# A one-core attention and two-layer FFN kernel: two transpose groups of each head pair moved to another place in TensorE's order

## The chip, the cores and the metric

The kernel runs on one core of a Trainium2 chip. The metric is the device time of one execution in microseconds; the time of a kernel is the median of its runs.

## The reference

The attention takes 4 batches of 8 heads, 576 positions and a head size of 64. Its scores carry a decay made of the running sum of log f, and its mask is causal. Two dense layers follow it, in fp32 throughout.

```python
scores = scale * np.matmul(q, k.transpose(0, 1, 3, 2))
cum = np.cumsum(np.log(np.clip(f, 0.0001, 1.0)), axis=-1)
scores = np.where(causal, -1e9, scores + cum[:, :, :, None] - cum[:, :, None, :])
attn = np.exp(scores - np.max(scores, axis=-1, keepdims=True))
attn = attn / (np.sum(attn, axis=-1, keepdims=True) + 1e-09)
x = np.matmul(attn, v)                  # then (tokens 2304, model 512)
h = x @ w_in;  x = (h - np.tanh(h)) @ w_out
h = x @ w_in2; out = (h * (1 / (1 + np.exp(-h)))) @ w_out2
```

## The kernel before

The attention takes two heads at a time, a **pair**; there are 16 pairs (`NP`). The 576 queries of a head are cut into blocks of 128 (the last of 64), which makes 9 score tiles for a pair (`NTILE`): blocks 0 to 3 of either head, and the last 64 queries of both heads in one tile. The tiles are made in four **units**: unit 0 is blocks 0 and 1 of both heads, units 1 and 2 are blocks 2 and 3, unit 3 is the last queries.

For each pair there are these pieces of work:

- `scores(p, u)` is TensorE's matmuls of a unit, K rows 0 to 63 for one head beside rows 64 to 127 for the other (unit 3 uses all 128 rows). The result tile `s` has two buffers in PSUM, so the scores of a unit need the buffer that the scores two units earlier filled.
- `least` is VectorE's reading of one score tile (L671): it adds the mask, finds the row's least value and writes the scores to SBUF. `expo` is the exponential on ScalarE (L679). `guard` and `normalise` (L686, L690 on VectorE, L693 on GpSimd) divide three tiles by their row sums.
- `transposes(p, u)` turns the finished tiles of a unit on TensorE (L705) into PSUM tiles `t`, of which there are three buffers (`ps_t`); `evac(p, u)` copies these to the SBUF tile `ptf`, some on ScalarE and some on VectorE (L750).
- `values(p)` multiplies the turned tiles with v (L761), and `collect` copies the result to `x`.

The order on every engine is written out by hand. The loop at L897 goes through steps n, nine for a pair; `later(n, fn, ...)` books a piece of work for a step, and `run(n, fn)` at the step writes it out. Scores of pair p+1 are written in the steps 8 (unit 0, the step before the pair's first), 0, 4 and 6 of the pair's nine; the transposes of pair p, which run while pair p+1's scores are made, in step 4 (unit 0, booked at `n0 + 13`), 6 (units 1 and 3's tile, `n0 + 15`) and 8 (unit 2, `n0 + 17`), each evacuated one step later; `values(p)` in step 4 of pair p+2. Within a step the order is transposes, values, scores, then evacuations, `expo`, `collect`, `least`, `normalise`, and last the jobs that prepare the first FFN weights (`wjob`, from pair 3 on one job each in the steps 1, 3, 5 and 7, most of them on VectorE). An engine takes its instructions in the order in which they are written, so the order of the steps is also the order on each engine.

The attention takes the first 170 us or so; the FFN's projections follow, in which TensorE works without a break.

Of the kernel before, what the change touches and what calls it, by code (L numbers as in the profile page):

```python
# [41 lines left out]
def forgetting_attention_two_ffn(  # L42
# [163 lines left out]
    for s in range(2 * NSET):  # L206
        e, o, k = 2 * s + 2, 2 * s + 3, 6 * s
# [104 lines left out]
    for u, (l, s, b) in enumerate(units):  # L312
# [14 lines left out]
        if l and s == 0:  # L327
            k = 5 if b == 0 else 11
# [208 lines left out]
    def attention(first):  # L537
        with ExitStack() as actx:
# [19 lines left out]
            NP = B * NPAIR  # L558
# [108 lines left out]
            def least(t):  # L667
                p, h, i = t
                src, m, pt = sps.pop(t)
                mn = small.tile([P, 1], F32, tag="mn", name=f"mn{p}_{h}_{i}")  # L670
                nc.vector.tensor_tensor_reduce(  # L671
                    out=pt.rearrange("p (g c) -> p g c", g=2) if i == 4 else pt, in0=src, in1=m,
                    op0=ALU.add, op1=ALU.min, scale=-SCALE, scalar=3.0e38, accum_out=mn,
                )
                ptile[t] = (pt, mn)

            def expo(n):
                pt, mn = ptile[tiles[n]]
                nc.scalar.activation(  # L679
                    pt, pt, AF.Exp, bias=mn, scale=-1.0,  # L680
                    accum_out=sums[:, n // 3 % 5, n % 3, 0:1],
                )

            def guard(n):
                sm = rowsum[n // 3] = small.tile([P, 3], F32, tag="sm", name=f"sm{n}")
                nc.vector.tensor_reduce(sm, sums[:, n // 3 % 5], axis=AX.X, op=ALU.add)  # L686

            def normalise(n):
                sm = rowsum.pop(n // 3)
                nc.vector.reciprocal(sm, sm)  # L690
                for j in range(3):
                    pt, _ = ptile[tiles[n + j]]
                    nc.gpsimd.tensor_scalar(pt, pt, sm[:, j:j + 1], 1.0, ALU.mult, ALU.mult)  # L693

            def transposes(p, u):

                ptf = ptfs[p % 2]
                tps[p, u] = moves = []
                both = u == 1 and p < NP - 1

                def tile(j):
                    return ps_t.tile([P, 4, P], F32, tag="t", name=f"t{p}_{u}_{j}")

                def turn(t, k, pt, c):
                    nc.tensor.transpose(t[:, k], pt[:, c * P:c * P + P], ident)  # L705

                def move(eng, src, dst):
                    moves.append((nc.scalar.copy if eng == "A" else nc.vector.tensor_copy, dst, src))

                def square(i, c, n, t, k, eng):  # L710
                    for h in range(2):
                        for j in range(n):
                            turn(t, k + n * h + j, pts[h, i], c + j)
                    src, q = t[:, k:k + 2 * n], P * i + 448 * c
                    if n == 1:
                        return move(eng, src, ptf[:, :, q:q + P])
                    dst = ptf[:, :, q:q + 448 * n].rearrange("p h (c w) -> p h c w", w=448)[:, :, :, 0:P]
                    move(eng, src.rearrange("p (h c) w -> p h c w", h=2), dst)

                def last_four(t, eng):  # L720
                    for c in range(4):
                        turn(t, c, pt4[p % 2], c)
                    dst = ptf[:, :, 512:512 + 4 * 448].rearrange("p h (c w) -> p c h w", w=448)[:, :, :, 0:64]
                    move(eng, t.rearrange("p c (h w) -> p c h w", h=2), dst)

                def last_fifth(t, k, eng):
                    turn(t, k, pt4[p % 2], 4)
                    o = 448 * 4 + 512
                    move(eng, t[:, k].rearrange("p (h w) -> p h w", h=2), ptf[:, :, o:o + 64])

                pts = {t: ptile.pop((p,) + t)[0] for t in units[u]}
                if both:
                    ptile.pop((p, 2, 4))
                if u == 0:
                    square(1, 0, 2, tile(0), 0, "V")
                    square(0, 0, 1, tile(1), 0, "A")
                elif u < 3:
                    square(u + 1, 0, 2, tile(0), 0, "A")
                    t = tile(1)
                    square(u + 1, 2, u, t, 0, "V")  # L740
                    if both:
                        last_fifth(t, 2, "V")
                        last_four(tile(2), "A")
                else:
                    last_four(tile(0), "A")
                    last_fifth(tile(1), 0, "V")

            def evac(p, u):
                for fn, dst, src in tps.pop((p, u)):
                    fn(dst, src)  # L750
# [35 lines left out]
            def busy(t, count):  # L786

                for _ in range(count):
                    nc.tensor.matmul(out_t, t[:, 0:P], t[:, 0:512], start=True, stop=True)  # L789
# [25 lines left out]
            def later(n, fn, *a):  # L815
                due.setdefault(max(n, 0), []).append((fn, a))

            def run(n, *fns):
                for fn, a in due.get(n, []):
                    if fn in fns:  # L820
                        fn(*a)

            for p in range(1, NP):
                n0 = NTILE * (p - 1)
# [12 lines left out]
            for p in range(NP):  # L837
                n0 = NTILE * p
                for u, k in enumerate((-1, 0, 4, 6)):
                    if p + u:  # L840
                        later(n0 + k, scores, p, u)
                k = ends_.get(p, steps_)
                for u in range(4 if k[3] else 3):
                    later(n0 + k[u], transposes, p, u)
                    later(n0 + k[u] + 1, evac, p, u)
                later(n0 + k[4], values, p, [(0, 0), (64, 0), (64, 1), (64, 2), (64, 3), (64, 4)])
                later(n0 + k[4] + 1, collect, p, 0, 64)
                later(n0 + k[4] + 1, collect, p, 64, S)

            def has(n):  # L850
                return 0 <= n < N
# [45 lines left out]
            for n in range(N + NTILE + 1):  # L897
                if n % NTILE == 0:
                    run(n, scores)
                    run(n, transposes)  # L900
                    run(n, values)
                else:
                    run(n, transposes)
                    run(n, values)
                    run(n, scores)
                if n < NTILE - 1:
                    busy(kqs[0][:, 0], 2)
                run(n, evac)
                if has(n - 1):
                    expo(n - 1)  # L910
                run(n, collect)
                if n % 3 == 2 and has(n - 5):
                    guard(n - 5)
                if has(n):
                    least(tiles[n])
                if n % 3 == 2 and has(n - 5):
                    normalise(n - 5)
                run(n, load_kq, load_v, split, place_last, place_dec, place_dec_last)
                for fn, *a in ahead.get(n - N, []):
                    fn(*a)  # L920
# [3 lines left out]
    with tc.manual_schedule():  # L924
        slots = [slot_steps(sl) for sl in range(NSL)]
        attention(slots[0])
        for job in jobs(1, 1, LAST):
            wjob(*job)
        for slot in slots:
            for _ in slot:  # L930
                pass
        rest()
        for n in range(8 * (NSL - 2) + 2, len(halves)):
            project(n)
# [39 lines left out]
```

## Time and profile before

| | before |
|---|---|
| median of 3 runs | 937.5 us (937.47 to 937.91) |
| profiled execution | 937.38 us |
| its span, first to last instruction | 935.6 us |
| TensorE busy | 927.4 us, 99% of the span |
| VectorE, ScalarE, GpSimd busy | 729.6, 439.0, 174.0 us |
| granted TensorE clock | 1.00 |
| period of a pair in the attention | 9.89 us |

Read the table from the stage: TensorE is busy nearly the whole span, and in the attention VectorE, ScalarE and GpSimd are nearly as full. A pair's period is the distance between the first matmul of unit 2 in one pair and that in the next.

### The profile page before, as it was taken

To read this page: it belongs to the slowest core of one execution; us is meant where nothing else is said; L and a number is where in the kernel's file an instruction comes from. 1 tells how busy PE (TensorE), PEld (TensorE's weight loads), DVE (VectorE), ACT (ScalarE), POOL (GpSimd) and SP (SyncE) were. 2 spreads that over 40 slices of the span, in tenths; PEclk is the share of its full clock that TensorE was granted. 3 is DMA by queue.
4 is the path that set the end of the run, shared out by engine and by line. 5 is a ranking of instruction groups with operands and counts; after the bars stand their busy time and mean duration, and the time that the engine had idled before them with its cause. 6 is when DMAs were issued, how large, how long until landed. Compare 5 with 4: busy or idle time off the path is not lost.

```text
span 935.6 us, 14919 instructions
## 1 busy us (share of the span) xinstructions
PE 927.4 (99%) x5532; PEld 846.0 (90%) x5532; DVE 729.6 (78%) x1320; ACT 439.0 (47%) x790; POOL 174.0 (19%) x248
## 2 busy tenths in 40 slices
PE   8999999999999999999999999999999999999998
PEld 6777777799999999999999999888888989888887
DVE  7798998898888887888788998877776677664444
ACT  6889888666453424242424354645342334232311
POOL 8999998200000000000000011010000000000000
PEclk9999999999999999999999999999999999999999
DMA  5435451668457753775477337464875477436722
GB/s 166 148 97 173 141 158 57 259 235 325 192 204 282 274 196 133 286 273 201 143 272 280 139 144 281 180 257 171 326 271 170 177 269 255 142 126 232 255 83 102
DMA packets 45946, 188.89 MB, mean 202 GB/s; under 512 B 9456, under 2 KB 9712, under 8 KB 45840
## 3 DMA queue, kind: packets, MB, share of 16 engines
q1 hardware_dynamic: 45720, 187.77, 55.0%
q8 instruction: 44, 0.72, 0.3%
q14 instruction: 30, 0.25, 0.1%
q10 hardware_dynamic: 152, 0.15, 0.1%
HBM read 148.44 MB, written 38.34 MB: 200 GB/s over the span
## 4 chain that ended last, share of the span: by engine, by line
PE 95%; DVE 3%; issue 1%; ACT 1%; POOL 0%; DMA 0%; POOLq 0%; ACTq 0%
PE a L385 42%; PE h L417 34%; PE t L705 5%; PE s L658 5%; PE out_t L761 4%; PE s L650 2%; PE h L431 2%; DVE xt L267 0%; PE out L761 0%; PE out_t L789 0%; DVE xo L281 0%; DVE wl L193 0%; DVE t L438 0%; PE a L367 0%; DVE gl L460 0%
## 5 line engine op out<-in xcount | busy, mean ns | idle before, releaser
L417 PE MATMUL h<-xo,wh 128*128 128x384 f32 x1232 | 314.0, 335 | 0.0
L470 DVE TENSOR_TENSOR hs<-h,hs 128x384 f32<-128x384 f32 x308 | 170.8, 555 | 90.3 <-PE h L417 86.6
L417 PEld LDWEIGHTS h<-xo,wh 128*128 128x128 f32 x1232 | 225.5, 188 | 14.1
L447 ACT ACTIVATE t<-hs 128x768 f32<-128x768 f32 x88 | 74.6, 847 | 309.2 <-DVE hs L470 309.2
L417 PE MATMUL h<-xo,wl 128*128 128x384 f32 x616 | 206.8, 336 | 0.0
L385 PE MATMUL a<-gh,wh 128*128 128x384 f32 x384 | 128.5, 335 | 0.5 <-ACT x L399 0.5
L385 PE MATMUL a<-gh,wl 128*128 128x384 f32 x384 | 128.3, 334 | 0.0
L385 PE MATMUL a<-gl,wh 128*128 128x384 f32 x384 | 128.3, 334 | 0.0
L460 DVE TENSOR_TENSOR gl<-t,gh 128x768 fp32r<-128x768 f32 x96 | 91.6, 954 | 34.0 <-ACT gh L456 33.6
L417 PEld LDWEIGHTS h<-xo,wl 128*128 128x128 f32 x616 | 115.6, 188 | 0.0
L385 PE MATMUL a<-wh,gl 128*128 128x512 f32 x284 | 112.6, 396 | 0.0
L385 PE MATMUL a<-wl,gh 128*128 128x512 f32 x284 | 112.2, 395 | 0.0
L385 PE MATMUL a<-wh,gh 128*128 128x512 f32 x284 | 110.5, 389 | 0.0
L456 ACT CAST gh<-t 128x768 fp32r<-128x768 f32 x96 | 80.4, 838 | 34.1 <-DVE t L449 27.9
L281 POOL TENSOR_TENSOR xo<-xt,xo 128x768 fp32r<-128x768 f32 x3 | 6.2, 2073 | 426.6 <-ACT xo L280 426.6
L679 ACT ACTIVATE p<-p,mn 128x128 f32<-128x128 f32 (+3 forms) x128 | 71.2, 558 | 16.9 <-DVE mn L671 14.2
L693 POOL TENSOR_SCALAR p<-p,sm 128x128 f32<-128x128 f32 (+3 forms) x128 | 72.7, 584 | 7.4 <-DVE sm L690 6.9
L385 PEld LDWEIGHTS a<-gh,wh 128*128 128x128 f32 x384 | 72.1, 188 | 1.1 <-ACT x L399 0.9
L385 PEld LDWEIGHTS a<-gl,wh 128*128 128x128 f32 x384 | 72.1, 188 | 0.0
L385 PEld LDWEIGHTS a<-gh,wl 128*128 128x128 f32 x384 | 72.1, 188 | 0.0
L671 DVE CUSTOM_DVE_ANT_0 p<-s,mask 128x128 f32<-128x128 f32 (+3 forms) x128 | 59.7, 480 | 14.3 <-PE s L658 14.2
L401 DVE TENSOR_TENSOR x<-a,x 128x768 f32<-128x768 f32 (+2 forms) x60 | 57.1, 951 | 9.2 <-PE a L385 9.1
(104 smaller groups left out, 1390.9 us busy)
## 6 DMA issues: line engine op xcount, KB each, us to landing
xo<-xd SPq DMA_DIRECT2D x126, 768.0 KB
xd<-xo SPq DMA_DIRECT2D x42, 768.0 KB
raw<-w_in SPq DMA_DIRECT2D x32, 512.0 KB
raw<-w_out SPq DMA_DIRECT2D x32, 512.0 KB
kqraw<-kq SPq DMA_DIRECT2D x16, 608.0 KB
vraw<-v SPq DMA_DIRECT2D x16, 320.0 KB
out<-ob SPq DMA_DIRECT2D x6, 512.0 KB
out<-ob SPq DMA_DIRECT2D x5, 256.0 KB
```

The source lines that it names most:

```text
L385: nc.tensor.matmul(dst, w, m, start=first and r == 0, stop=last and r == 2)
L401: nc.vector.tensor_tensor(total, acc, total, ALU.add)
L417: nc.tensor.matmul(dst, w[:, ks], m[:, k], start=k == 0 and r == 0, stop=k == 1 and r == 2)
L447: nc.scalar.activation(t, hs[h], AF.Silu if l else AF.Tanh)
L456: nc.scalar.copy(gh, hs[h])
L460: nc.vector.tensor_tensor(gl, hs[h], rd(gh), ALU.subtract)
L470: nc.vector.tensor_tensor(to, p, s, ALU.add)
L658: nc.tensor.matmul(s[:, h, c:c + n], a[half(h), q], b[half(h), 0:n], start=r == 0, stop=r == 3,)
L671: nc.vector.tensor_tensor_reduce(out=pt.rearrange("p (g c) -> p g c", g=2) if i == 4 else pt, in0=src, in1=m, op0=ALU.add, op1=ALU.min, sc ...
L679: nc.scalar.activation(pt, pt, AF.Exp, bias=mn, scale=-1.0, accum_out=sums[:, n // 3 % 5, n % 3, 0:1],)
L693: nc.gpsimd.tensor_scalar(pt, pt, sm[:, j:j + 1], 1.0, ALU.mult, ALU.mult)
L705: nc.tensor.transpose(t[:, k], pt[:, c * P:c * P + P], ident)
```

## The change

For every pair but the last two, the transposes of unit 0 are booked in the step of unit 1's (`k[1]`, step 6) under another name, `turn_first`, which `run` writes behind the evacuations of that step. For this the evacuation of unit 1 comes one step earlier, into the step of its own transposes, and the evacuation of unit 0 goes to the step after, two steps later than before.

```diff
+            def turn_first(p, u):
+                transposes(p, u)
+
@@
                 for u in range(4 if k[3] else 3):
+                    if p < NP - 2 and u < 2:
+                        later(n0 + k[1], (turn_first, transposes)[u], p, u)
+                        later(n0 + k[1] + 1 - u, evac, p, u)
+                        continue
                     later(n0 + k[u], transposes, p, u)
                     later(n0 + k[u] + 1, evac, p, u)
@@
                 run(n, evac)
+                run(n, turn_first)
                 if has(n - 1):
                     expo(n - 1)
```

Instructions are the same in number and kind; their order differs. In the rows below, `s5_2` is the scores of pair 5, unit 2, `t4_0_1` the second PSUM tile of pair 4's unit 0 transposes, `p5_2` and `pt4` the score tiles in SBUF, `mn` the row minima, `out_0` and `out_t` the results of the values.

TensorE, at the end of pair 5's unit 1 scores, before:

```order
L658 MATMUL s5_1_992<-de1_108 128x384 x2
L705 MATMUL t4_0_0_1033<-ident_203,p4_0_791 128x128 x4
L705 MATMUL t4_0_1_1038<-ident_203,p4_0_791 128x128 x2
L761 MATMUL out_0_3_1041<-ptf1_105,vraw3_669 64x64 x2
L761 MATMUL out_t_113<-ptf1_105,vraw3_669 64x512 x2
L761 MATMUL out_t_113<-ptf1_105,vraw3_669 64x448 x2
```

and with the change:

```order
L658 MATMUL s5_1_992<-de1_108 128x384 x2
L764 MATMUL out_0_3_1033<-ptf1_105,vraw3_669 64x64 x2
L764 MATMUL out_t_113<-ptf1_105,vraw3_669 64x512 x2
L764 MATMUL out_t_113<-ptf1_105,vraw3_669 64x448 x2
L764 MATMUL out_t_113<-ptf1_105,vraw3_669 64x320 x2
```

The values of pair 3 now stand directly behind the scores; the six transposes of pair 4's unit 0 are gone from between them.

TensorE, at the end of pair 5's unit 3 scores, before:

```order
L650 MATMUL s5_3_1098<-de1_108,lq1_110 128x288
L705 MATMUL t4_2_0_1118<-ident_203,p4_2_886 128x128 x4
L705 MATMUL t4_2_1_1123<-ident_203,p4_2_886 128x128 x4
L658 MATMUL s6_0_1128<-kqs6_990 128x128 x6
L658 MATMUL s6_0_1128<-de0_107 128x128 x2
```

and with the change:

```order
L650 MATMUL s5_3_1088<-de1_108,lq1_110 128x288
L705 MATMUL t4_0_0_1101<-ident_203,p4_0_791 128x128 x4
L705 MATMUL t4_0_1_1106<-ident_203,p4_0_791 128x128 x2
L705 MATMUL t4_2_0_1118<-ident_203,p4_2_878 128x128 x4
L705 MATMUL t4_2_1_1123<-ident_203,p4_2_878 128x128 x4
L658 MATMUL s6_0_1128<-kqs6_990 128x128 x6
L658 MATMUL s6_0_1128<-de0_107 128x128 x2
```

The six transposes now stand here, between the last queries' scores and the transposes of unit 2.

VectorE, from the reading of pair 5's unit 2 scores (`s5_2`) to that of its unit 3 (`s5_3`), before:

```order
L671 ISA p5_2_1055,mn5_0_3_1108<-s5_2_1054,mask_152 128x512
L671 ISA mn5_0_3_1108 128x1
L750 COPY ptf0_106<-t4_1_1_1089 128x2x128
L750 COPY ptf0_106<-t4_1_1_1089 128x2x64
L671 ISA p5_2_1055,mn5_1_3_1115<-s5_2_1054,mask_152 128x512
L671 ISA mn5_1_3_1115 128x1
L179 TENSOR_TENSOR ws0_0_1016<-ws0_0_1016 128x256
L686 TENSOR_REDUCE sm48_1147<-sums_157 128x3
L671 ISA pt4_1_112,mn5_2_4_1149<-s5_3_1098,mask4_159 128x576
L671 ISA mn5_2_4_1149 128x1
```

and with the change:

```order
L753 COPY ptf0_106<-t4_1_1_1079 128x2x128
L753 COPY ptf0_106<-t4_1_1_1079 128x2x64
L671 ISA p5_2_1047,mn5_0_3_1110<-s5_2_1046,mask_152 128x512
L671 ISA mn5_0_3_1110 128x1
L753 COPY ptf0_106<-t4_0_0_1101 128x2x2x128
L671 ISA p5_2_1047,mn5_1_3_1115<-s5_2_1046,mask_152 128x512
L671 ISA mn5_1_3_1115 128x1
L179 TENSOR_TENSOR ws0_0_1016<-ws0_0_1016 128x256
L686 TENSOR_REDUCE sm48_1147<-sums_157 128x3
L671 ISA pt4_1_112,mn5_2_4_1149<-s5_3_1088,mask4_159 128x576
L671 ISA mn5_2_4_1149 128x1
```

The copies of `t4_1_1` now stand ahead of both readings of `s5_2` rather than between them, and the copy of `t4_0_0` has come between the two (before it stood two tiles earlier, between the two readings of `s5_1`). On ScalarE the copies of `t4_1_0` and `t4_1_2` likewise stand one exponential earlier, and that of `t4_0_1` two later.

## Rows read from the trace of the kernel before

**Rows 1.** The page, part 1: engine, busy us, share of the span, instructions.

```profile
PE 927.4 (99%) x5532; PEld 846.0 (90%) x5532; DVE 729.6 (78%) x1320; ACT 439.0 (47%) x790; POOL 174.0 (19%) x248
```

**Rows 2.** Pairs' periods: total, busy PE, PEld, DVE, ACT, POOL; clock, DMA.

```profile
32.02:41.93 9.91, 9.91 (x93) 7.47 (x89) 7.76 (x30) 8.65 (x24) 9.17 (x15) 1.00 0.58 190
...
61.70:71.59 9.89, 9.89 (x93) 7.46 (x89) 9.79 (x36) 8.42 (x27) 9.81 (x16) 1.00 0.26 81
...
sum 128.55, PE 128.55 PEld 96.96 DVE 116.61 ACT 109.07 POOL 124.56; mean PE 9.89 PEld 7.46 DVE 8.97 ACT 8.39 POOL 9.58
```

**Rows 3.** All waits of TensorE, 0 to 230 us: total, times, longest.

```profile
PE out_t L789 <- POOL de L781: 1.8, 1, 1.8
PE t L705 <- POOL pt L693: 0.9, 1, 0.9
```

**Rows 4.** TensorE in time order, 62 to 73 us: start, us, line, out<-in, forms.

```profile
63.54 0.71 PE L705 MATMUL t<-ident,pt 128*128 128x128 f32 x5
...
65.15 1.04 PE L705 MATMUL t<-ident,p 128*128 128x128 f32 x8
66.12 0.55 PE L658 MATMUL s<-kqs 64*128 64x128 f32 x6
...
67.14 0.69 PE L658 MATMUL s<-kqs 64*128 64x384 f32 x6
67.66 0.34 PE L658 MATMUL s<-de 64*128 64x384 f32 x2
67.93 0.87 PE L705 MATMUL t<-ident,p 128*128 128x128 f32 x6
68.74 0.34 PE L761 MATMUL out<-ptf,vraw 128*64 128x64 f32 x4
...
73.43 0.71 PE L705 MATMUL t<-ident,pt 128*128 128x128 f32 x5
```

**Rows 5.** VectorE in time order, 63 to 68 us, the same stretch.

```profile
63.07 0.68 DVE L671 CUSTOM_DVE_ANT_0 p<-s,mask 128x512 f32<-128x512 f32 x1
...
63.85 0.62 DVE L750 COPY ptf<-t 128x256 f32<-128x256 f32 x2
64.39 0.68 DVE L671 CUSTOM_DVE_ANT_0 p<-s,mask 128x512 f32<-128x512 f32 x1
...
65.00 0.77 DVE L179 TENSOR_TENSOR ws<-ws 128x256 f32<-128x256 f32 x1
65.69 0.15 DVE L686 TENSOR_REDUCE sm<-sums 128x3 f32<-128x6 f32 x1
65.76 0.74 DVE L671 CUSTOM_DVE_ANT_0 pt<-s,mask 128x576 f32<-128x576 f32 x1
66.43 0.08 DVE L671 DVE_READ_ACCUMULATOR2_ANT mn<- 128x1 f32 x1
...
67.22 0.67 DVE L750 COPY ptf<-t 128x512 f32<-128x512 f32 x1
67.82 0.28 DVE L671 CUSTOM_DVE_ANT_0 p<-s,mask 128x128 f32<-128x128 f32 x1
```

**Rows 6.** GpSimd, first pair: normalising its last query rows.

```profile
23.11 0.74 POOL L693 TENSOR_SCALAR pt<-pt,sm 128x576 f32<-128x576 f32 x1
```

**Rows 7.** TensorE, first pair: the transposes that waited for it.

```profile
23.90 0.77 PE L705 MATMUL t<-ident,pt 128*128 128x128 f32 x5 [0.93 <-POOL pt L693]
```

**Rows 8.** VectorE, first pair: the evacuation behind these transposes.

```profile
24.27 0.62 DVE L750 COPY ptf<-t 128x256 f32<-128x256 f32 x2 [1.09 <-PE t L705]
```

**Rows 9.** GpSimd: the same normalising in the pairs of Rows 4.

```profile
62.12 0.75 POOL L693 TENSOR_SCALAR pt<-pt,sm 128x576 f32<-128x576 f32 x1
...
71.55 0.74 POOL L693 TENSOR_SCALAR pt<-pt,sm 128x576 f32<-128x576 f32 x1
```

**Rows 10.** VectorE, 45 us: first of nine weight jobs in that place.

```profile
45.23 0.43 DVE L159 TENSOR_SCALAR wa<-raw 128x512 uint32<-128x512 uint32 x1
```

**Rows 11.** VectorE, 154 us: the last of the nine.

```profile
153.98 0.61 DVE L179 TENSOR_TENSOR ws<-ws 128x256 f32<-128x256 f32 x1
```

## The prediction

> **What bounds the kernel now.** I read the page's shares first, then the stage that the change touches by its stretches, then TensorE's waits, then the engines in time order. The page says that TensorE is busy 99% of the span [rows 1]; that is an average over attention and projections, so it doesn't say what may be moved for nothing. In the attention a pair takes 9.89 us, and TensorE is busy for all of it, at a granted clock of 1.00, the upper of its two levels (2.4 GHz) [rows 2]. Beside it GpSimd is busy 9.58 us of 9.89 on the mean and VectorE 8.97, and in single pairs 9.8 both [rows 2]. TensorE's waits in the attention are one in the first pair, 0.9 us on GpSimd [rows 3], and none behind it. So TensorE's own order sets the pace now, and the three others keep up by little: VectorE is idle for 128.55 - 116.61 = 11.9 us in thirteen pairs [rows 2]. A change to TensorE's order can win only what its own switches cost, and it can lose wherever it makes an engine with so little to spare stand still.
>
> **What TensorE wins.** The transposes themselves cost the same in either place: five take 0.71 us and eight 1.04, so 0.11 apart, and one alone 0.27 [rows 4]. What differs is the switch of shape. Ahead of the transposes stand matmuls on 64 rows; these 384-column pairs start (67.66 - 67.14)/3 = 0.17 apart, but from the last to the first transpose it is 67.93 - 67.66 = 0.27, and from there to the first matmul of the values 0.81 [rows 4]. Together 1.08 us, of which 6 x 0.11 = 0.66 is paid again behind the last queries' scores (all 128 rows, like the transposes). That leaves 0.42, less the direct step from scores to values, which no row shows. Its bounds are 0.17, as if it were no switch, and 0.27, as from scores to transposes; I take 0.27, because it is as much a change of shape. The gain is 0.15 us, at most 0.25, for each of the 13 pairs whose values now follow scores: 2.0 us, at most 3.2.
>
> The Trainium skill (TensorEngine Tiling (Array Packing), Key Properties) says that changing the tiling mode drains TensorE, a rule in favour of this change, since one change of mode in five goes for each pair. The 0.27 against 0.17 agrees with it. By that rule alone the kernel would come out faster, which is the first rival below.
>
> In the first pair the front place was free. Its transposes stood ahead of a wait for GpSimd that ended at 23.90 [rows 7], right behind the normalising (23.11 + 0.74 = 23.85) [rows 6], which the change leaves where it is. There the 0.66 is new cost.
>
> **What TensorE loses: the chain through VectorE.** VectorE's copy of the first moved PSUM tile now stands between the two readings of the unit 2 scores, and the second reading is what frees the score buffer for the next pair's unit 0. In the pair of [rows 5], count from the first transpose behind the last queries' scores. The tile's fourth transpose ends at 3 x 0.11 + 0.27 = 0.60 [rows 4]. VectorE starts 0.04 later (a transpose started at 23.90 and lasted some 0.33, the copy starts at 24.27) [rows 7, 8]. The copy holds it for 67.82 - 67.22 = 0.60, the reading for 65.00 - 64.39 = 0.61 and 0.08 for its row minimum [rows 5]. TensorE goes on 0.05 behind its releaser (23.90 against 23.85) [rows 6, 7]. Sum: 1.98 us. Without a wait TensorE would be there after 66.12 - 65.15 = 0.97 for eight transposes, and 0.66 for six more: 1.63 [rows 4]. So it waits 0.35 us, in each of 14 pairs: 4.9 us. The wait for a free transposes' buffer, which also comes into being there, lies inside these 0.35. VectorE can't be earlier: it ends the first reading near 65.1 (63.85 + 0.54 for the copies now ahead of it, the start of the next row, + 0.69) and the tile is there only at 65.15 + 0.64 = 65.79 [rows 4, 5].
>
> Chain, switches and first pair: 4.9 - 2.0 + 0.7 = 3.6 us.
>
> **What is queued behind.** Behind the second reading stand, on VectorE, a weight job and then the reading of the last queries' scores, which frees the buffer for unit 1 of the next pair. Before, the job was covered: the reading ended at 66.51 and unit 1 started at 67.14 [rows 4, 5]. Now unit 0 starts 0.05 behind the second reading's end and unit 1 wants to start 67.14 - 66.12 = 1.02 later [rows 4]. The job J, the row sums' 0.07, the last reading's 0.74 or so and 0.05 of handing over go into the same time [rows 5], so TensorE waits J - 0.21. Nine pairs have such a job on VectorE there, with rows of 0.43 us at first [rows 10] and 0.61 at last [rows 11]; the one shown here, 0.77, holds the engine for 65.69 - 65.00 = 0.69 [rows 5], 0.08 less than its row. Over the nine that makes 5.3 us, less 9 x 0.21: 3.4 us. Its lower bound is zero, if the jobs get shorter where GpSimd isn't at work beside them.
>
> **What GpSimd adds.** The transposes of the last queries want the tile that GpSimd normalises as its last for the pair. That ends at 62.87 and 72.29 [rows 9], and TensorE comes at 63.54 and 73.43 [rows 4]: 0.67 and 1.14 to spare. TensorE's way there is now shorter by the 0.81 that stood ahead; the first of the two is then 0.14 late, the second not. Bounds: zero, since GpSimd gets time whenever TensorE waits elsewhere, and 13 x 0.81 = 10.5 if all of it shows, because VectorE, which starts GpSimd's work, is later too. I take 0.18 a pair, near the one that is short: 2.3 us.
>
> The sum is 3.6 + 3.4 + 2.3 = 9.3 us. The profiled execution took 937.4 us, 0.1 under the median of the runs, with 1.8 outside its span; the change doesn't touch that, nor the projections, where nothing is idle that could give time back. So **946.7 us**.
>
> A second way to the same place, by VectorE's budget: the copies make it stand still for 63.85 - 63.07 = 0.78 and for 65.79 - 65.1 = 0.7 in each pair [rows 4, 5]. With its work of 8.97 on the mean that is 10.4 us instead of 9.89, or 0.56 x 13 = 7.3 us, and in a pair with 9.79 of work 1.4 us more [rows 2]; with the first pair's 0.7 it is 8. The Trainium skill (TensorE: Matmul & The Clock Gate, Architectural detail) says that VectorE's and ScalarE's queues are strict FIFO, a rule against this change: a copy that waits for TensorE holds all that is behind it. The rows agree in that what is written behind is never started earlier.
>
> **The rivals.** *First, faster or no change: the switches decide.* If VectorE's stops are covered by its 11.9 us of idle time, only the gain is left: 937.4 - 2.0 + 0.7 = 936.1, or 934.9 with the upper 3.2. For it: the idle time is real, and now it is spent waiting for the same scores. Against it: the 0.35 is a chain from TensorE to VectorE and back, which no idle time elsewhere shortens; it would decide only if copy and reading together took 0.35 less than their 1.2 us. A measurement of this kernel tells about 0.2%, 1.9 us, from no change; this case lies on both sides of that.
>
> *Second, the chain alone.* The jobs and GpSimd hide themselves behind the new waits: 937.4 + 3.6 = 941.0. For it: each wait of TensorE gives the others time. Against: VectorE's and GpSimd's heaviest pairs have 0.1 us to spare [rows 2].
>
> *Third, VectorE or GpSimd becomes the bound.* Then the stops come on top of full pairs: 1.45 us in each of 13 less only the idle time of the light pairs, some 5 of the 11.9 us, is 14, so about 951 to 954. For it: VectorE's 9.79 and GpSimd's 9.81 of 9.89 [rows 2]. Against: the light pairs, such as one with 7.76, can't be slowed by it beyond the chain.
>
> **How the numbers follow.** The forecast, 943 to 950, has 0.58. The chain alone has 0.17, the third 0.18. The first rival has 0.07, of which 0.03 for faster by over 0.2% and 0.04 for within it. Slower by over 0.2% is 0.93. The range of 941.5 to 952 leaves out the first rival, the lower half of the second and the upper half of the third, some 2 in 10.
>
> **What would show it.** In the profile after, TensorE should have new waits of 0.35 in all in every pair, at the next pair's unit 0 scores on VectorE and perhaps in part inside the transposes, at a PSUM buffer; at unit 1's scores where a job stands; and at the last queries' transposes on GpSimd. A period without a job should be near 10.1 us. VectorE should idle some 0.7 us ahead of the copy of the moved tile. The step from scores to values should be 0.27. Wrong it would be if periods were under 9.89, or if VectorE had no idle time ahead of that copy.

## The result and the profile after

With the change the kernel takes 951.1 us (four runs, 950.94 to 951.31) against 937.7 for the kernel before (four runs beside them, 937.47 to 937.96): 1.0145 times as long, with a 95% interval of 1.0133 to 1.0157. That is 13.4 us more, where 9.3 were forecast; 951.1 lies inside the range of 941.5 to 952, near its upper end, and above the 943 to 950 that was held likeliest. The profiled execution took 950.94 us with a span of 949.1, at a granted clock of 1.00, so 1.8 us lie outside the span, as before.

The page of the kernel after: engine, busy us, share and instructions (part 1), then the shares by engine of the chain that ended last (part 4).

```profile
PE 933.8 (98%) x5532; PEld 846.7 (89%) x5532; DVE 727.5 (77%) x1320; ACT 440.8 (46%) x790; POOL 171.8 (18%) x248
...
PE 87%; POOL 5%; DVE 4%; issue 1%; DMA 1%; ACT 1%; POOLq 0%; SPq 0%; DVEq 0%; ACTq 0%
```

Beside [rows 1] the work on each engine is almost the same: VectorE 727.5 us for 729.6, ScalarE 440.8 for 439.0, GpSimd 171.8 for 174.0. TensorE's 933.8 is higher by 6.4, for the same matmuls: a run of transposes with a wait inside it, or a matmul that restarts behind a wait, is shown longer. No engine got more to do; they wait for one another. The chain shows with whom: for 5% of the span it goes through GpSimd and for 4% through VectorE. Before, it was 0% and 3%:

```profile
PE 95%; DVE 3%; issue 1%; ACT 1%; POOL 0%; DMA 0%; POOLq 0%; ACTq 0%
```

TensorE's waits in the attention (engine, line, operation waited for; total us, times, longest), to be read against [rows 3]:

```profile
PE t L705 <- POOL pt L693: 5.8, 9, 1.0
...
PE s L658 <- DVE mn L671: 1.2, 4, 0.7
```

Nine waits for GpSimd's last normalising, where there was one, and four for a reading of VectorE. One of these, the longest, is the first pair's (below), three are at a next pair's unit 1 scores. An idle time counts from the modelled end of the matmul in front, which is some 0.16 us later than the next one could start (six transposes are shown as 0.87 us, though the next can start 0.71 behind their start), so what a wait costs is read from starts. This is one pair on TensorE, the counterpart of [rows 4] (start, us, line, out<-in, forms, count, idle before):

```profile
64.99 0.87 PE L705 MATMUL t<-ident,p 128*128 128x128 f32 x6
66.62 0.76 PE L705 MATMUL t<-ident,pt 128*128 128x128 f32 x5 [0.75 <-POOL pt L693]
...
68.28 1.94 PE L705 MATMUL t<-ident,p 128*128 128x128 f32 x14
70.27 0.55 PE L658 MATMUL s<-kqs 64*128 64x128 f32 x6
...
71.35 0.79 PE L658 MATMUL s<-kqs 64*128 64x384 f32 x6
71.98 0.34 PE L658 MATMUL s<-de 64*128 64x384 f32 x2
72.25 0.34 PE L764 MATMUL out<-ptf,vraw 128*64 128x64 f32 x4
```

The transposes of the last queries want to start 0.71 behind 64.99, at 65.70; they start at 66.62, 0.92 late, on GpSimd. The run of 14 transposes, eight before, goes from 68.28 to the next scores at 70.27, 1.99 instead of 0.97 + 0.66 = 1.63. From scores to values it is 72.25 - 71.98 = 0.27.

Two pairs' periods (us, then busy time of PE, PEld, DVE, ACT and POOL, clock, DMA), to stand beside [rows 2]; the first has neither a weight job in unit 1's place nor a wait for GpSimd, the second is the pair above:

```profile
32.26:42.36 10.10, 10.02 (x93) 7.45 (x91) 6.72 (x27) 7.97 (x24) 8.72 (x15) 1.00 0.45 137
63.87:75.10 11.23, 10.40 (x93) 7.50 (x90) 9.49 (x35) 8.29 (x26) 9.75 (x16) 1.00 0.23 70
```

10.10 us is the period that the change alone makes: 9.89 + 0.36 - 0.15. Of the 14 pairs only this one has it; the others go up to 11.77, and one engine's busy time doesn't explain them: in the second pair none but TensorE is busy for more than 9.75 of 11.23.

The same stretch on VectorE, the counterpart of [rows 5]:

```profile
68.91 0.69 DVE L753 COPY ptf<-t 128x512 f32<-128x512 f32 x1 [0.70 <-PE t L705]
69.52 0.68 DVE L671 CUSTOM_DVE_ANT_0 p<-s,mask 128x512 f32<-128x512 f32 x1
...
70.13 0.42 DVE L179 TENSOR_TENSOR ws<-ws 128x256 f32<-128x256 f32 x1
70.47 0.15 DVE L686 TENSOR_REDUCE sm<-sums 128x3 f32<-128x6 f32 x1
70.54 0.75 DVE L671 CUSTOM_DVE_ANT_0 pt<-s,mask 128x576 f32<-128x576 f32 x1
...
71.21 0.17 DVE L690 RECIPROCAL sm<-sm 128x3 f32<-128x3 f32 x1
```

VectorE waits 0.70 us for the moved tile, copies it, and only then reads unit 2's second tile (69.52), does its job (L179), reads the last queries' scores (70.54), and makes the reciprocals (71.21) that stand behind this reading. On those GpSimd waits, some 6 us ahead of TensorE's wait for GpSimd. Here is GpSimd from the end of the pair before:

```profile
60.32 1.60 POOL L693 TENSOR_SCALAR p<-p,sm 128x256 f32<-128x256 f32 x3 [1.68 <-DVE sm L690]
61.88 1.13 POOL L592 TENSOR_SCALAR kqs<-kqraw 128x576 fp32r<-128x576 f32 x1
63.09 0.80 POOL L600 TENSOR_TENSOR kqs<-kqraw,kqs 128x288 fp32r<-128x288 f32 x1
63.88 1.81 POOL L693 TENSOR_SCALAR p<-p,sm 128x512 f32<-128x512 f32 x2
65.65 0.91 POOL L693 TENSOR_SCALAR pt<-pt,sm 128x576 f32<-128x576 f32 x1
```

It stood still for 1.68 us up to 60.32, because VectorE's reciprocals came so late, then worked without a gap until 65.65 + 0.91 = 66.56, and TensorE went on at 66.62. Waits of this kind on GpSimd (30 to 162 us before, 30 to 172 after, the same work):

```profile
POOL p L693 <- DVE sm L690: 2.4, 5, 0.7
```

```profile
POOL p L693 <- DVE sm L690: 15.7, 11, 1.7
```

Two more waits of the kernel after, of 1.3 and 1.1 us, are put down to ScalarE by the profile. They too end 0.17 us behind the end of the reciprocals, as all the others do, so they are of the same kind.

From starts as above each pair's excess over 9.89 us can be split, and summed over the 14 pairs. The 0.66 of transposes that moved is taken out of both places.

| part, us over the 14 pairs | forecast | measured |
|---|---|---|
| chain through VectorE (run of transposes to unit 0's scores) | 4.9 | 5.1 |
| jobs (unit 1's scores) | 3.4 | 2.3 |
| GpSimd's tile (last queries' transposes), less the 1.15 of before | 2.3 | 7.3 |
| a wait of the values in one pair | – | 0.2 |
| switch of shape gone | -2.0 | -2.0 |
| front place lost in the first pair | 0.7 | 0.7 |
| sum | 9.3 | 13.5 |

So the sum misses in one place above all, GpSimd. The experiments ask why.

### The profile page after: what moved, and what is told of

It reads as the page before. It is cut to its first block, busy times and chain, and to the rows that moved or that the text cites. A ratio compares the mean times of both kernels' runs of the same rounds, so it can differ in the third digit from the quotient of the medians.

```text
span 949.1 us, 14870 instructions
## 1 busy us (share of the span) xinstructions
PE 933.8 (98%) x5532; PEld 846.7 (89%) x5532; DVE 727.5 (77%) x1320; ACT 440.8 (46%) x790; POOL 171.8 (18%) x248
## 4 chain that ended last, share of the span: by engine, by line
PE 87%; POOL 5%; DVE 4%; issue 1%; DMA 1%; ACT 1%; POOLq 0%; SPq 0%; DVEq 0%; ACTq 0%
PE a L385 41%; PE h L417 34%; PE s L658 3%; PE out_t L764 3%; PE t L705 2%; POOL p L693 2%; PE h L431 2%; PE s L650 1%; POOL kqs L600 1%; POOL pt L693 1%; DVE ptf L753 1%; DVE p L671 1%; DMA lq<-kqs 1%; POOL kqs L592 1%; DVE xt L267 0%
## 5 line engine op out<-in xcount | busy, mean ns | idle before, releaser
L693 POOL TENSOR_SCALAR p<-p,sm 128x128 f32<-128x128 f32 (+3 forms) x128 | 70.3, 567 | 23.6 <-DVE sm L690 20.1
```

## The experiments

The table at the end of this section splits every run in the same way. A ratio is against the kernel before on the same chip, with its 95% interval.

**E1 and E2: each of VectorE's two stops by itself.** VectorE stands still ahead of unit 1's copy and ahead of the moved tile's. Each copy is written in its turn at the end of the step, behind the readings and the job:

```diff
+            def evac_late(p, u):
+                evac(p, u)
@@ e1
-                        later(n0 + k[1] + 1 - u, evac, p, u)
+                        later(n0 + k[1] + 1 - u, (evac_late, evac)[u], p, u)
@@ e2
+                        later(n0 + k[1] + 1 - u, (evac, evac_late)[u], p, u)
@@ e2: turn_first is written behind evac_late too
                     fn(*a)
+                run(n, evac_late)
```

> The change, with the copies of unit 0's PSUM tiles written at the end of their step: on VectorE behind the second reading of unit 2's scores and behind the weight job, no longer between the two readings. TensorE's order is that of the change, instruction for instruction. Theory V (VectorE's stop between the two readings makes the loss): the wait ahead of the next pair's unit 0 scores falls from 0.36 us a pair to the 0.16 or so that ScalarE's copy of the second tile still costs, the weight jobs no longer delay unit 1's scores, the row sums' reciprocals come some 0.7 us earlier and GpSimd's lateness (7.3 us) falls by more than half: 940 to 943. Rival P (the place of the transposes on TensorE makes it: GpSimd's tile is wanted 0.8 us earlier, and seven PSUM tiles in a run go through three buffers): the copies' place changes little, 948 to 951.

> The change, with unit 1's copies written behind the first reading of unit 2's scores, as before the change, instead of ahead of it. This takes away the first of VectorE's two stops in a pair and leaves the second, the copy of unit 0's tile between the two readings. If both stops cost (the budget of my prediction, 0.78 and 0.7 us a pair), half the loss goes: 944 to 946. If the second stop alone sets the time (VectorE waits there for the same transposes anyway, only 0.7 us longer), nothing changes: 950 to 952. Rival P: nothing changes either.

E1 (the moved tile's copy late): 944.5 us, 1.0076 (1.0059 to 1.0093). E2 (unit 1's copies late): 951.4 us, 1.0149 (1.0129 to 1.0169). E1 takes half away, GpSimd's part (7.3 to 3.8 over before) and the whole jobs' part, but lands between what the two theories wanted. E2 takes nothing. VectorE in E2, the same place in its second pair:

```profile
34.43 0.62 DVE L756 COPY ptf<-t 128x256 f32<-128x256 f32 x2
36.37 0.69 DVE L756 COPY ptf<-t 128x512 f32<-128x512 f32 x1 [1.32 <-PE t L705]
```

Unit 1's copy waits no more, and ahead of the moved tile's it now waits 1.32 us where it was 0.70: the stop in front was time that VectorE would have waited anyway. Two stops before the same event don't add up. That fells the prediction's second way, by VectorE's budget, which added 0.78 and 0.7.

**E3: both copies late.** Both edits together.

> The change, with both: unit 1's copies behind the first reading, unit 0's behind the second reading and the job. TensorE's order is that of the change. Theory V: VectorE has no stop of over 0.3 us in a pair without a job, the reciprocals come as early as before the change, and TensorE keeps 0.16 us a pair of waiting for ScalarE's copy, which eats the 0.15 of the switch: 938 to 941, with periods of 9.9 us in pairs with little work. Rival P: TensorE still waits for GpSimd, as its tile is wanted 0.8 us earlier all the same: 945 or more.

944.2 us, 1.0072 (1.0057 to 1.0087): neither theory's value. VectorE waits 5.6 us for transposes instead of 24.8, and still TensorE waits for GpSimd in five pairs beside the first (the row counts the four longer ones), 3.3 us in all over before; the rest is the chain, 4.4, at another link: ScalarE's copy. The waits of TensorE, VectorE (30 to 172 us) and GpSimd (30 to 166 us) in E3:

```profile
PE t L705 <- POOL pt L693: 3.0, 5, 1.0
```

```profile
DVE ptf L756 <- PE t L705: 5.6, 11, 0.7
```

```profile
POOL p L693 <- DVE sm L690: 6.7, 10, 1.2
```

GpSimd's waits for reciprocals have gone from 15.7 to 6.7 us. So VectorE's stops make about half of GpSimd's part; the other half must have another reason. Two are at hand. TensorE asks for the tile 0.81 us earlier, and GpSimd has 0.3 of 9.89 us to spare [rows 2]. And GpSimd's last normalising itself takes longer where VectorE's jobs run beside it: over the 14 pairs 10.7 us before, 13.5 after and 13.6 in E3, in one pair 1.71 instead of 0.74. No run separates the two.

**E4: a part of the change alone.** Unit 1's copies one step earlier, in the kernel before; the transposes stay.

```diff
-                    later(n0 + k[u] + 1, evac, p, u)
+                    later(n0 + k[u] + (u != 1 or p >= NP - 2), evac, p, u)
```

> The kernel before, with one part of the change alone: unit 1's copies come one step earlier, ahead of the first reading of unit 2's scores. The transposes stay where they were before. Theory V: VectorE's stop of 0.78 us a pair is covered by its 11.9 us of idle time and by the 0.67 us and more that the next step has to spare, so 937.5 to 939. If the earlier copies of unit 1 by themselves made VectorE and GpSimd late: 941 or more.

938.9 us, 1.0014 (1.0004 to 1.0025). Alone this part costs some 1.1 us, all of it at unit 1's scores. It is the moved tile that matters.

**E5: the reciprocals first.** In the kernel after, the sums and reciprocals are written ahead of the reading of the last queries' scores:

```diff
                     guard(n - 5)
+                    normalise(n - 5)
                 if has(n):
                     least(tiles[n])
-                if n % 3 == 2 and has(n - 5):
-                    normalise(n - 5)
```

> The change, with one thing more: the reciprocals of the row sums, and GpSimd's normalising behind them, are written ahead of VectorE's reading of a score tile in their step instead of behind it. TensorE's order and the copies are those of the change. If GpSimd is late because VectorE's stops hold the reciprocals back (GpSimd waited 15.7 us for them in the run of the change), they come some 0.75 us earlier here, TensorE's waits for GpSimd's tile fall from 7.3 us to 3 or 4, and the first pair wins up to 1 us: 946 to 948. If GpSimd is late by its own pace alone, only the first pair wins: 950 to 951.

945.0 us, 1.0081 (1.0061 to 1.0101). TensorE's waits in E5 have no row with GpSimd's tile any more, not even that of the first pair; this one is left:

```profile
PE s L658 <- DVE mn L671: 2.2, 4, 0.8
```

(Of its 2.2 us one wait of 0.8 is the first pair's, as after.) The reciprocals come some 0.7 us earlier, by the length of the reading that stood ahead of them; GpSimd still waits for them, 11.2 us in all, but no longer so long that TensorE is reached. GpSimd's part falls from 8.4 to nothing, further than expected, so earlier reciprocals are enough to make GpSimd punctual. Something else changes with them: its last normalising no longer meets VectorE's jobs and takes 0.74 to 0.76 us in every pair, in the pair with 1.71 too. GpSimd in E5:

```profile
83.99 0.75 POOL L693 TENSOR_SCALAR pt<-pt,sm 128x576 f32<-128x576 f32 x1
```

The reading now pays: it starts 0.2 us later, and the jobs' part goes from 2.3 to 4.4.

**E6: the jobs elsewhere.** The fourth place of the weight jobs is put one step later, `(1, 3, 5, 7)` to `(1, 3, 5, 8)`.

> The change, with the weight jobs of step 7 moved to step 8, behind the reading of the last queries' scores and the reciprocal. The 2.3 us at unit 1's scores should vanish whatever else is true, and the reciprocals come earlier by the job's 0.35 to 1.0 us in nine pairs. If the reciprocals' lateness makes GpSimd late: another 1.5 to 3 us less, 945.5 to 947.5. If it doesn't: 948.5 to 949.

950.9 us, 1.0144 (1.0124 to 1.0164): a miss. The 2.3 us at unit 1's scores vanish, as expected, but GpSimd's part rises by 1.9. TensorE's and GpSimd's waits in E6, then VectorE's reciprocals ahead of GpSimd's 60.32 in the kernel after, then in E6 the same reciprocals and GpSimd's normalising behind them:

```profile
PE t L705 <- POOL pt L693: 7.6, 10, 1.2
```

```profile
POOL p L693 <- ACT p L679: 14.5, 14, 1.3
```

```profile
59.98 0.17 DVE L690 RECIPROCAL sm<-sm 128x3 f32<-128x3 f32 x1
```

```profile
59.39 0.17 DVE L690 RECIPROCAL sm<-sm 128x3 f32<-128x3 f32 x1
59.73 2.15 POOL L693 TENSOR_SCALAR p<-p,sm 128x256 f32<-128x256 f32 x3 [1.06 <-ACT p L679]
```

The profile names ScalarE's exponentials here, but all 14 waits still end 0.17 to 0.19 us behind the end of the reciprocals, as in the kernel after (60.32 against 60.15, 59.73 against 59.56). The reciprocals do come earlier, 0.59 us in this pair. GpSimd loses that again: its three tiles take 2.15 us instead of 1.60, with the moved job now beside them, and they end at 61.88 for 61.92. So its last tile comes no earlier, and TensorE, which has lost its wait at unit 1's scores, asks for it earlier and waits longer.

**E7 and E8: less work for GpSimd.** In E7 the rounding copy of a pair's k and q goes from GpSimd to ScalarE; E8 is E3 with that edit.

```diff
-                    if p == 0:
+                    if p == 0 or j == 0:
                         nc.scalar.copy(hi[:, c], raw[p][:, c])
```

> The change, with GpSimd relieved of one instruction a pair: the high half of k (the copy of 576 columns at L592, 0.67 to 1.1 us, which stands ahead of the normalising of the tile that TensorE waits for) is copied by ScalarE. VectorE's stops and TensorE's order are those of the change. If the tile comes late because GpSimd has no time to spare behind VectorE's stops: TensorE's waits for it fall from 7.3 to 2 or 3 us, and the chain of 0.36 us a pair and the 2.3 us at unit 1's scores stay: 946 to 947.5. If ScalarE, with that work added, becomes late for its own copies: more wait at the transposes' buffers, 949 or more.

> The third run (both copies behind the readings) and the seventh together. What was left there was 3.3 us of waits for GpSimd's tile in five pairs, and a chain of 0.10 us a pair net of nothing else. If those 3.3 us are TensorE asking 0.8 us earlier for a tile of a GpSimd without slack, they go, and the first pair's wait too: 939.5 to 941.5. If they stay, the place of the transposes costs something that GpSimd's load does not explain: 943.5 to 944.5.

E7: 945.6 us, 1.0087 (1.0066 to 1.0107). E8: 941.6 us, 1.0045 (1.0028 to 1.0062). TensorE's waits for GpSimd's tile, E7 and then E8:

```profile
PE t L705 <- POOL pt L693: 1.4, 2, 1.2
```

```profile
PE t L705 <- POOL pt L693: 0.6, 2, 0.5
```

With 0.7 us a pair less to do, GpSimd bears the late reciprocals (its waits for them are even longer, 17.2 us) and is on time in most pairs: its part falls from 8.4 to 2.0, and 1.4 of these stand in the one pair in which the last normalising still takes 1.71 us. With E3's order as well 1.1 is left. What remains of E8 is the chain, 4.6.

**E9 to E12: what the change could give.** If the chain can be taken out, the 2.0 us of the switch should show. Here ScalarE's copies are written where the change put them, VectorE's at the end of the step, the moved group's small tile ahead of its large one, and the first pair is left out. E9 has E5's edit with that, E10 that of E7. E11 and E12 are the kernel before with E5's and E7's edit, so that these are not taken for a gain of the change.

```diff
@@ e9, e10
-                    if p < NP - 2 and u < 2:
+                    if 0 < p < NP - 2 and u < 2:
                         later(n0 + k[1], (turn_first, transposes)[u], p, u)
-                        later(n0 + k[1] + 1 - u, evac, p, u)
+                        later(n0 + k[1] + 1 - u, evac_late, p, u)
+                        later(n0 + k[1] + 1 - u, evac_act, p, u)
@@ in transposes, for u == 0 and these pairs
-                    square(1, 0, 2, tile(0), 0, "V")
-                    square(0, 0, 1, tile(1), 0, "A")
+                        square(0, 0, 1, tile(1), 0, "A")
+                        square(1, 0, 2, tile(0), 0, "V")
```

> A reworked change, to see whether the switch's 0.15 us a pair can be had at all: the transposes stand where the change puts them (but for the first pair, whose front place was free), VectorE's copies behind the readings and the job as in the third run, ScalarE's copies in the change's places, the two-column tile turned ahead of the four-column one so that its buffer is free sooner, and the row sums ahead of the reading as in the fifth run. If TensorE's waits for VectorE, GpSimd and the buffers all go, periods are 9.74 and the time 934.5 to 936, the first pair's 1 us included. If GpSimd or ScalarE stays late in the full pairs: 937 to 940.

> The same rework, with the split's high half on ScalarE (as in the seventh run) instead of the row sums ahead of the reading. Where GpSimd's load was the rest of the loss: 934.5 to 936.5. Where ScalarE's added load makes its copies late: 938 to 941.

> The kernel before with the row sums ahead of the reading, as a control for the ninth run. TensorE waits for nothing there but 0.9 us in the first pair, so it wins at most that: 936.3 to 936.6. If the readings that now come later delay the next scores in pairs with a job: 937 to 939.

> The kernel before with the split's high half on ScalarE, as a control for the tenth run: the first pair's wait for GpSimd may shrink by 0.7 us, nothing else is waited for: 936.7 to 937.5.

E9: 937.3 us, 0.9999 (0.999 to 1.0007). E10: 937.6, 1.0002 (0.9993 to 1.0011). E11: 936.7, 0.9993 (0.9984 to 1.0001). E12: 937.4, 0.9999 (0.9991 to 1.0008). None beats the kernel before by what can be told, and neither E9 nor E10 comes to the 934.5 to 936.5 hoped for; E11 is the nearest, with the first pair's 0.9 us gone from its trace. In E9 a light pair on TensorE:

```profile
40.38 0.97 PE L658 MATMUL s<-kqs 64*128 64x512 f32 x6
...
43.82 1.69 PE L705 MATMUL t<-ident,p 128*128 128x128 f32 x14
45.44 0.55 PE L658 MATMUL s<-kqs 64*128 64x128 f32 x6
...
50.12 0.96 PE L658 MATMUL s<-kqs 64*128 64x512 f32 x6
```

The period is 50.12 - 40.38 = 9.74, 0.15 under the 9.89 of before, and from the first of 14 transposes to the next scores it is 1.62. So the gain of the switch is real and the chain can be taken out. But against that 9.74 two pairs lose 0.6 and 0.7 at unit 1's scores, three 0.2 there and two 0.2 elsewhere, and the 2.0 are gone. E10 loses 1.4 in one pair, the one with the normalising of 1.71 us.

What each run lost, in us over its 14 pairs against 9.89 us, from starts in TensorE's timeline ("chain" is from the run of transposes to unit 0's scores; the first pair's 1.15 of before is in its column; the 0.7 of the first pair's lost front place, in the kernel after and in all of E1 to E8 but E4, has none):

| run | time | GpSimd's tile | chain | unit 1's scores | values | switch |
|---|---|---|---|---|---|---|
| before | 937.7 | 1.15 | 0 | 0 | 0 | 0 |
| after | 951.1 | 8.41 | 5.13 | 2.27 | 0.20 | -1.98 |
| E1 moved tile's copy late | 944.5 | 4.92 | 4.48 | 0.03 | 0 | -1.95 |
| E2 unit 1's copies late | 951.4 | 8.51 | 5.19 | 2.26 | 0.19 | -1.96 |
| E3 both late | 944.2 | 4.43 | 4.35 | 0.04 | 0 | -1.95 |
| E4 before, unit 1's copies early | 938.9 | 1.16 | 0 | 1.13 | 0 | 0 |
| E5 reciprocals first | 945.0 | 0 | 5.15 | 4.37 | 0.17 | -1.97 |
| E6 jobs a step later | 950.9 | 10.28 | 5.12 | 0.01 | 0.41 | -1.95 |
| E7 less for GpSimd | 945.6 | 1.98 | 5.15 | 2.60 | 0.19 | -1.98 |
| E8 E3 and E7 | 941.6 | 1.08 | 4.59 | 0.03 | 0 | -1.95 |
| E9 rework, reciprocals first | 937.3 | 0.10 | 0.34 | 1.79 | 0.22 | -1.96 |
| E10 rework, less for GpSimd | 937.6 | 1.91 | 0.13 | 0.39 | 0.20 | -1.95 |

## Why the prediction was right, and where it wasn't

**The sign and the bound.** That TensorE's order has little to win and much to lose held. The first rival, switches alone, is out: the new waits cost more than seven times what the switches gave. VectorE's 11.9 us of idle time [rows 2] were no reserve for a chain that runs from TensorE to VectorE and back.

**The switch: right.** The step from scores to values, for which no row stood and 0.27 was chosen between 0.17 and 0.27, is 0.27 in all 13 pairs: the gain is 0.15 each, and E9's period of 9.74 shows it alone. The Trainium skill (TensorEngine Tiling (Array Packing), Key Properties) has a change of mode drain TensorE; the rows agree, and one change less in a pair is worth 2 us in 938.

**The first pair's 0.66: right, for a nearer reason too.** Its unit 2 scores start at 20.97 us, with the six transposes gone from in front of them, and at 20.96 before, with them. TensorE waits there for VectorE instead. TensorE before, then after:

```profile
20.96 0.98 PE L658 MATMUL s<-kqs 64*128 64x512 f32 x6
```

```profile
20.97 0.97 PE L658 MATMUL s<-kqs 64*128 64x512 f32 x6 [0.72 <-DVE mn L671]
...
23.94 0.77 PE L705 MATMUL t<-ident,pt 128*128 128x128 f32 x5 [0.97 <-POOL pt L693]
```

The front place gave nothing back, here already and not only at GpSimd's tile, which comes at 23.94 for 23.90 [rows 7].

**The chain: right in size, and partly in another place.** 0.36 us a pair against 0.35. About 0.24 of it lies inside the run of transposes, which takes 1.94 us, against 1.69 in E9: there TensorE waits for a PSUM buffer that ScalarE must empty. ScalarE in the pair above, its copy of the small moved tile (unit 0's second); the transposes go on 0.05 us behind its end:

```profile
69.13 0.37 ACT L753 COPY ptf<-t 128x256 f32<-128x256 f32 x1 [0.52 <-PE t L705]
```

The prediction had placed this wait inside the 0.35 and the end of the chain on VectorE, and the end is right. But with VectorE's copy out of the way (E3, E8) the buffer's 0.24 stays in eleven pairs, with 0.3 to 0.8 in the other three, so removing one link doesn't remove the wait. Both links have to go, as in E9 and E10, where 0.34 and 0.13 us are left of 5.1.

**The jobs: mis-sized, 2.3 for 3.4.** The rule was a wait of J less 0.21; J was too long. Six of the nine jobs now hold VectorE for 0.34 us and three for 0.61 (rows of 0.42 and 0.69), 3.9 us in all where 5.3 were taken from the trace before. 3.9 - 9 x 0.21 = 2.0. The 0.21 was too short as well: the job starts beside the reading's row minimum, 0.08 us before that ends, so each wait is that much shorter. Of the 2.3 measured, 1.3 are such late starts and the rest is the restart, which the prediction left out: scores that had to wait take 0.1 us longer, 0.79 for six at 71.35 above where [rows 4] has 0.69. The L179 job is one of them: 0.77 in [rows 5], beside a GpSimd at work, and 0.42 at 70.13 above, while GpSimd waits. This is the lower bound's own reason, that jobs get shorter where GpSimd stands still.

**GpSimd: the step that failed, 7.3 for 2.3.** The prediction took 0.18 a pair, near the one pair that it found short, and its lower bound was that "GpSimd gets time whenever TensorE waits elsewhere". That time was no use to it: GpSimd works on what VectorE hands it, and VectorE's reciprocals stand behind the very reading that the moved copy delays. The prediction followed that delay to TensorE's unit 1 scores and not to the reciprocals behind the same reading, though it said of the upper bound that VectorE, "which starts GpSimd's work, is later too". Its 1.68 us of waiting in one pair turn up as TensorE's 0.92 in the next. Nor did the prediction ask whether the normalising would keep its 0.74 us in another place; it takes 2.8 us more over the 14 pairs. No share can be given to one cause alone, since each relief removes half or more of the same 7.3: the reciprocals 0.7 us earlier (E5) all of it, 0.7 us less work for GpSimd (E7) most, VectorE without its stops (E1, E3) half. That TensorE asks 0.81 us earlier was not tried by itself; it is argued from what E3 leaves and E8 takes away, and E8 shortens the normalising in most pairs too. The bounds of 0 and 10.5 held 7.3; the choice went to the pair that was 0.14 late instead of asking what GpSimd itself waits for. That 951.1 still lies in the range is in part luck: GpSimd came out 5.0 over the forecast and the jobs 1.1 under it.

**The second way: wrong.** 7 to 8 us by adding VectorE's two stops a pair was near the forecast by accident: E2 removes the first stop and the time stays the same.

**The third rival: its time without its mechanism.** It gave 951 to 954 if VectorE or GpSimd became the bound. The time is 951.1, but neither is: in the attention VectorE waits for transposes and GpSimd for reciprocals, 24.8 and 15.7 us (30 to 172 us).

```profile
DVE ptf L753 <- PE t L705: 24.8, 26, 2.4
```

What bounds those pairs is a ring of waits through four engines in a handwritten order: TensorE's transposes, VectorE's copy and reading, its reciprocals, GpSimd's normalising, TensorE's next transposes. In the pair above the ring closes: from GpSimd's start at 60.32 round to the same start in the next pair it takes 11.23 us, which is the period. Each engine has idle time; the ring has none there.

```profile
71.55 1.60 POOL L693 TENSOR_SCALAR p<-p,sm 128x256 f32<-128x256 f32 x3 [1.39 <-DVE sm L690]
```

**What stays open.** Why two pairs of E9 lose 0.6 and 0.7 us at unit 1's scores was not followed further, nor how much of GpSimd's part its longer normalising makes by itself, nor whether an order exists that keeps all of the 2.0.

## What to carry to other kernels

When a copy is moved on an in-order engine, follow every instruction behind it on that engine to its reader, not only the one that TensorE waits for: here the cost was less in the reading that was delayed than in the reciprocals, one instruction of 0.17 us, written behind it. An engine that is 97% busy doesn't gain from another's wait unless its input is there by then; ask first what it waits for itself. And stops ahead of the same event don't add: take the later one.

## What the hardware showed that was not expected

A job on VectorE with two tensors can take twice as long or more when GpSimd is at work. The L166 job takes 0.69 us in the kernel after while GpSimd waits (for 1.68 us up to 60.32, above), and 1.42 in E3, where GpSimd works from 53.88 to 57.94 without a gap. VectorE after, then VectorE and GpSimd in E3:

```profile
58.63 0.69 DVE L166 SCALAR_TENSOR_TENSOR wb<-raw,wb 128x512 f32<-128x512 uint32 x1
```

```profile
55.48 1.42 DVE L166 SCALAR_TENSOR_TENSOR wb<-raw,wb 128x512 f32<-128x512 uint32 x1
...
66.30 1.15 DVE L179 TENSOR_TENSOR ws<-ws 128x256 f32<-128x256 f32 x1
```

```profile
53.88 2.46 POOL L600 TENSOR_TENSOR kqs<-kqraw,kqs 128x288 fp32r<-128x288 f32 x3
56.33 1.61 POOL L693 TENSOR_SCALAR p<-p,sm 128x128 f32<-128x128 f32 x3
```

The L179 job (66.30) goes from 0.42 to 1.15 us in the same two kernels. It works the other way round too: GpSimd's normalising of the last queries, 0.74 and 0.75 us in [rows 9], takes 1.71 in a pair of the kernel after in which VectorE does a two-tensor job of 1.28 us beside it. GpSimd and VectorE there:

```profile
86.91 1.71 POOL L693 TENSOR_SCALAR pt<-pt,sm 128x576 f32<-128x576 f32 x1
```

```profile
86.72 1.28 DVE L193 TENSOR_TENSOR wl<-ws,wh 128x1024 fp32r<-128x1024 f32 x1
```

The Trainium skill (GPSIMD Engine Reference, Specifications) names an interface to SBUF that GpSimd shares with VectorE and says that they contend, among other cases, when VectorE has two SBUF inputs. The rows agree, with a price of 0.7 us a job on one side and about 1 us on the other. It is not always VectorE that pays: in E6 the L166 job beside GpSimd's three tiles takes 0.68 us, and the tiles take 2.15 us instead of 1.60. VectorE in E6:

```profile
60.19 0.68 DVE L166 SCALAR_TENSOR_TENSOR wb<-raw,wb 128x512 f32<-128x512 uint32 x1
```

E6 comes nearest to a test, since it moves nothing but jobs; no run was made for this pairing alone, so that the shared interface is the cause is read from rows side by side and not tested.
